# Start of a convolution and SoLU layer: w_in's third block in one transfer, a band mask of one head, two multiplications on GpSimd, and another order of first products, sums and w_out's decode

## The chip, the cores and the metric

The kernel runs on one core of a Trainium2 chip. The core has five engines that each work through their own queue in program order: TensorE (PE: matmuls, with weight loads beside them, PEld), VectorE (DVE), ScalarE (ACT), GpSimd (POOL) and SyncE (SP, which here only issues DMAs). They wait for one another by semaphores. Sixteen DMA engines move data between HBM and the on-chip memory SBUF; matmuls write to PSUM. The metric is the device time of one launch in microseconds, lower is better.

## The reference

The first part is a causal convolution with 7 taps along the sequence, one softmax-normed set of taps for each of 8 heads of 24 channels. The second is a layer of width 1024 with a softmax-gated activation, a layer norm and an output product.

```python
# x [8, 4160, 192], weight [8, 7]
w = exp(weight - max(weight)); w = w / (sum(w) + 1e-09)
out = einsum('hk,bskhg->bshg', w, x_unf)        # 7 taps, causal
# w_in [192, 1024], w_out [1024, 192], g_ln [1024], doubles on entry
h = x @ w_in
e = exp(h - max(h)); sm = e / (sum(e) + 1e-09)
solu = h * sm
ln = (solu - mean(solu)) / sqrt(var(solu) + 1e-06) * g_ln
return ln @ w_out
```

There are 33280 rows, 260 tiles of 128. The weights arrive as 64-bit floats, which the kernel takes apart as pairs of 32-bit words.

## The kernel before

The kernel works on 17 chunks of the sequence (the first of 1024 rows, the second of 1056, the others of 2080) and, in the main loop, on three tiles of 128 rows at once (`three_steps`). For a tile, PE forms ph = y·w_in from fp16 halves (`whi` and `wlo` for w_in, upper and lower y in the transposed tile `yT`). DVE takes the row maximum (`emit_max`), ACT the exponential (`emit_exp`), DVE the numerator (`emit_mul`), ACT the upper half in fp16 (`emit_hi`), POOL the lower half (`emit_lo`), a DMA transposes it into `pT`, and PE multiplies by w_out (`ohl`). All this stands in one program order written by hand: an engine's queue is the order in which the code calls it, and what an engine can't start yet holds up all that is behind it on the same engine.

The change lies in what comes before the main loop:

- **Loads.** SP issues `weight`, then x of chunk 0 (`xr`) and w_in (`raw_in`) in turn. w_in has 192 rows: rows 0 to 127 come in two halves of 512 columns (L383), and rows 128 to 191, the third block, as two transfers over 64 partitions each (L388), side by side in columns 1024 to 1535 of the tile (slice `Z`; the two halves are `halves[0]` and `halves[1]`). Then w_out (`raw_out`, L392).
- **Taps.** POOL makes a 0/1 mask for all heads in `band` (L404, L405), DVE multiplies the taps in (L524), sums, and PE spreads them into `taps`.
- **Decode of 64-bit words** (class `Words`). DVE cuts out exponents (`exponents`, L447) and mantissas (`mantissas`, L452), adds the low word (`join`, L481); ACT turns exponents into powers of two (`powers`, L487) and sums their squares (`squares`, L470); DVE puts in the sign (`signs`, L490), and mantissa times power gives the value (`value`, L497). For w_in all multiplications are on DVE; for w_out the low words (`lows`, L458), the sum (`whole`, L475) and the value (L497) are on POOL, the conversion (`floats`, L464) on ACT.
- **Scales.** PE adds up the squares over partitions (`total`), DVE makes a power of two from the sum: `s` for x (from `xm`), `t_in` for w_in (from `isq`). `cv` holds products of both.
- **Convolution of chunk 0** in two parts: banks `pq` (windows 0 to 4) and `pr` (5 to 9). ACT writes the upper halves y (L313), DVE the lower (L322), and `settle` has SP transpose three blocks into `yT` (L352): block 0 needs uppers alone, block 2 the first two lowers, block 1 all.
- **fp16 halves of w_in.** ACT makes `whi` (L628 for the halves, L644 for the third block), DVE `wlo` (L647).
- **First tiles** (`first_two`, `emit_first`): tiles 0 and 1 share their first products; w_out is decoded between their steps, and `out_powers` multiplies the powers by g_ln on ACT (L685). Then `second_two`: tiles 2 and 3, two convolution products of chunk 1 in the banks of tile 1, w_out's mean over 1024 rows.

The engine of the last step of the decode is an argument:

```python
def value(self, c, powers, eng):
    f = self.f[:, c]
    eng.tensor_tensor(f, f, powers[:, c].bitcast(F32), ALU.mult)
```

Of the kernel before, what the change touches and what calls it, by code (L numbers as in the profile page):

```python
# [19 lines left out]
def kernel(  # L20
# [9 lines left out]
    nc = tc.nc  # L30
# [356 lines left out]
    for j in range(2):  # L387
        nc.sync.dma_start(  # L388
            raw_in[j * R : (j + 1) * R, F:, :].rearrange("p f t -> p (f t)"),
            w_in[2 * R : D, j * F : (j + 1) * F],  # L390
        )
# [12 lines left out]
    pool.memset(band, 1.0)  # L404
    pool.affine_select(  # L405
        out=band, in_=band, pattern=[[0, H], [-1, TB], [-1, K]],
# [101 lines left out]
    def valued(c):  # L508

        wi.signs(c, wi.m)  # L510
        wi.value(c, wi.m, dve)
# [13 lines left out]
        band, band, wb.unsqueeze(2).broadcast_to([TJ, H, TB, K]), ALU.mult  # L525
# [12 lines left out]
    valued(halves[0])  # L538
# [48 lines left out]
    isq = cp.tile([P, 2], F32, name="isq")  # L587
# [45 lines left out]
    wo.lows(W, 2.0**-32)  # L633
    wi.join(Z)
    valued(Z)
    for pc, hg in got0:
        c0.upper(pc, *hg)
# [35 lines left out]
    gate = cp.tile([1, 1], F32, name="gate")  # L673
# [67 lines left out]
    def emit_first(t, u):  # L741
# [4 lines left out]
        for j, w, r in ((0, whi, 0), (2, whi, 0), (0, wlo, 0), (1, whi, 1)):  # L746
            for q, lhs in zip((t, u), y):
                for n, bank in enumerate(banks_of(q)):
                    nc.tensor.matmul(
                        bank, lhs[j], w[:, r, n * 512 : (n + 1) * 512],  # L750
                        start=j == 0 and w is whi, stop=False,
                    )
                for n in range(NH if r else 0):
                    emit_third(q, n, False, False)
# [394 lines left out]
    def first_two():  # L1149
# [4 lines left out]
        emit_exp(t)  # L1154
        wo.signs(W, wo.e)

        pool.tensor_copy(gate, wo.e.bitcast(F32)[0:1, 0:1])
        wo.whole(W)
# [439 lines left out]
```

## Time and profile before

| | before |
|---|---|
| device time, three runs | 1162.87, 1164.15, 1164.42 us |
| median | 1164.15 us |
| profiled execution: span from first to last instruction | 1161.5 us |
| PE busy in the span | 1132.2 us (97%) |
| DVE, ACT, POOL busy | 1016.8, 998.0, 878.6 us |
| DMA: packets, bytes | 727391, 226.95 MB |

The profile is of one execution. Its own whole time is not listed; what is known is its span, and that the timed runs lie 1.4 to 2.9 us above it. In a timeline row stand start and length in us, the engine, the line of the kernel, the operation, what it writes and reads, the shape, how many were merged (x3), and in brackets how long the engine had been idle and what ended that. A row of a table by stretch has the stretch, its length, busy time and number of instructions of PE, PEld, DVE, ACT and POOL, the granted clock of PE (1.00 is full), the share of time the 16 DMA engines were busy and GB/s. "DMA to landing" is from the issue of a transfer to the arrival of its last byte.

### The profile page before, as it was taken

How to read it: one execution, taken by the hardware profiler on the slowest of the kernel's cores; microseconds unless marked ns; L12 is line 12 of the kernel's file. 1: busy time of each engine (PE TensorE's matmuls, PEld its weight loads, DVE VectorE, ACT ScalarE, POOL GpSimd, SP SyncE). 2: the span in 40 equal slices, each digit the busy share in tenths (PEclk: the TensorE clock that was granted, in tenths of full speed). 3: DMA queues.
4: the chain of work that ended last, by engine and by line, in shares of the span. 5: the costliest groups of instructions: out<-in, count | busy, mean ns of one | idle time of the engine just before them, and what ended most of it. 6: DMA issues, size and time to landing. Idle time of an engine off the chain costs nothing.

```text
span 1161.5 us, 22374 instructions
## 1 busy us (share of the span) xinstructions
PE 1132.2 (97%) x7742; PEld 692.4 (60%) x7742; DVE 1016.8 (88%) x2058; ACT 998.0 (86%) x1775; POOL 878.6 (76%) x686
## 2 busy tenths in 40 slices
PE   5898999999999999999999999999999999999998
PEld 3575566656666665655656666665666566566556
DVE  8888898988989898998889989888898988788787
ACT  6998988888888888888888888898888889888886
POOL 2745879987888588887868888588788858855665
PEclk9999999999999999999999999999999999999999
DMA  8799899999999999999999999999999998999988
GB/s 226 171 181 180 185 218 205 205 201 202 200 213 195 195 186 220 207 189 199 202 198 190 208 209 199 187 202 208 206 204 198 195 193 170 174 177 186 181 163 188
DMA packets 727391, 226.95 MB, mean 195 GB/s; under 512 B 651614, under 2 KB 725870, under 8 KB 727278
## 3 DMA queue, kind: packets, MB, share of 16 engines
q1 hardware_dynamic: 727278, 225.53, 100.2%
q8 instruction: 60, 0.98, 0.3%
q14 instruction: 53, 0.43, 0.1%
HBM read 33.00 MB, written 25.56 MB: 50 GB/s over the span
## 4 chain that ended last, share of the span: by engine, by line
PE 88%; DVE 5%; ACT 2%; DMA 2%; issue 2%; POOL 1%; SPq 0%; DVEq 0%; ACTq 0%; POOLq 0%
PE po L859 40%; PE ph L736 36%; PE pc L281 6%; PE ph L759 5%; DVE e L807 1%; DMA pT<-p 1%; DVE ph L790 1%; DMA raw_in<-in_moe_w_in_dram 1%; ACT e L797 1%; ACT sq L819 0%; DVE raw L869 0%; DVE y L322 0%; POOL p L827 0%; PE mean L701 0%; DVE wlo L647 0%
## 5 line engine op out<-in xcount | busy, mean ns | idle before, releaser
L827 POOL TENSOR_TENSOR p<-e,p 128x1024 f16<-128x1024 f32 x257 | 548.3, 2138 | 219.5 <-ACT p L815 218.0
L859 PE MATMUL po<-ohl,pT 128*128 128x192 f16 (+1 forms) x4264 | 539.8, 283 | 7.8 <-DVE raw L869 5.4
L859 PEld LDWEIGHTS <-pT 128*128 128x128 f16 x4264 | 384.4, 98 | 167.1 <-issue 7.6
L736 PE MATMUL ph<-whi,yT 128*128 128x512 f16 x1548 | 419.1, 380 | 2.7 <-DVE e L807 2.6
L790 DVE TENSOR_SCALAR_CACHE_REDUCE ph<-ph,cv 128x1024 f32<-128x1024 f32 x248 | 319.1, 1288 | 72.9 <-PE ph L759 56.6
L797 ACT ACTIVATE e<-ph,sm 128x1024 f32<-128x1024 f32 x260 | 289.4, 1113 | 102.0 <-DVE ph L790 95.8
L807 DVE SCALAR_TENSOR_TENSOR e<-ph,cv,e 128x1024 f32<-128x1024 f32 x248 | 317.1, 1279 | 26.0 <-ACT e L797 25.7
L736 PEld LDWEIGHTS <-yT 128*128 128x128 f16 x2064 | 192.6, 98 | 231.3 <-issue 36.3
L815 ACT CAST p<-e 128x1024 f16<-128x1024 f32 x257 | 266.8, 1039 | 27.9 <-DVE e L807 27.3
L819 ACT ACTIVATE sq<-e 128x1024 f32<-128x1024 f32 x260 | 273.4, 1052 | 0.2
L736 PE MATMUL ph<-wlo,yT 128*128 128x512 f16 x516 | 153.5, 379 | 0.0
L869 DVE TENSOR_REDUCE raw<-po 128x192 f32<-128x384 f32 x247 | 136.3, 552 | 14.3 <-PE po L859 13.9
L243 POOL TENSOR_TENSOR xs<-xr,xs 128x960 f16<-128x960 f32 (+1 forms) x56 | 107.6, 1922 | 1.4
L313 ACT ACTIVATE y<-pc 112x432 f16<-112x432 f32 (+5 forms) x140 | 62.8, 469 | 13.8 <-PE pc L281 8.1
L759 PE MATMUL ph<-wlo,yT 64*128 64x512 f16 x269 | 74.0, 380 | 0.0
L322 DVE SCALAR_TENSOR_TENSOR y<-pc,y 112x432 f16<-112x432 f32 (+5 forms) x140 | 72.2, 532 | 0.8 <-ACT y L313 0.8
L281 PE MATMUL pc<-xs,taps_hi 128*112 128x240 f16 (+1 forms) x448 | 72.9, 261 | 0.0
L759 PE MATMUL ph<-wlo,y 64*128 64x512 f16 x251 | 68.6, 380 | 0.0
L181 DVE TENSOR_REDUCE xa<-xr 128x1 f32<-128x384 f32 x112 | 66.6, 617 | 0.0
L281 PEld LDWEIGHTS <-taps_hi 128*112 128x112 f16 x448 | 52.4, 130 | 16.4
L240 POOL TENSOR_SCALAR xr<-xr,s 128x960 f32<-128x960 f32 (+1 forms) x56 | 57.5, 1027 | 2.9
L281 PE MATMUL pc<-xs,taps_lo 128*112 128x240 f16 (+1 forms) x224 | 58.5, 261 | 0.0
(148 smaller groups left out, 787.6 us busy)
## 6 DMA issues: line engine op xcount, KB each, us to landing
out_dram<-raw SPq DMA_DIRECT2D x127, 192.0 KB, 3.0
xr<-in_x_dram SPq DMA_DIRECT2D x41, 480.0 KB, 4.7
xr<-in_x_dram SPq DMA_DIRECT2D x22, 384.0 KB, 4.1
pT<-p SPq DMA_TRANSPOSE x263, 4.6
y<-yT SPq DMA_DIRECT2D x15, 140.0 KB, 3.1
y<-yT SPq DMA_DIRECT2D x15, 126.0 KB, 3.1
yT<-y SPq DMA_TRANSPOSE x102, 3.7
raw_out<-in_moe_w_out_dram SPq DMA_DIRECT2D x1, 1536.0 KB
```

Of the source, the lines that this page charges most:

```text
L243: (2.1 * size + 0.2, lambda: pool.tensor_tensor(xl, r, h, ALU.subtract)),
L281: nc.tensor.matmul(o, tp[:, h + j, :], r, start=q == 0, stop=q == len(ops) - 1)
L736: nc.tensor.matmul(bank, lhs, w[:, r, n * 512 : (n + 1) * 512], start=start and j == 0, stop=stop and j == len(ops) - 1,)
L759: nc.tensor.matmul(banks_of(t)[n], y[q, t.off : t.off + P], wlo[q, 1, n * 512 : (n + 1) * 512], start=start, stop=not start,)
L790: dve.tensor_scalar(t.ph, t.ph, t.cv[:, 0:1], None, ALU.mult, ALU.min, accum_out=t.bias)
L797: act.activation(t.e, t.ph, AF.Exp, bias=t.bias, scale=-1.0, accum_out=grp.z[:, g : g + 1])
L807: dve.scalar_tensor_tensor(t.e, t.ph, t.cv[:, 3:4], t.e, ALU.mult, ALU.mult, accum_out=t.grp.s1[:, t.g : t.g + 1],)
L815: act.copy(t.p16[:, :, 0, :], t.halves)
L819: act.activation(junk, t.e, AF.Square, accum_out=t.grp.s2[:, t.g : t.g + 1])
L827: eng.tensor_tensor(t.p16[:, :, 1, :], t.halves, t.p16[:, :, 0, :], ALU.subtract)
L859: nc.tensor.matmul(t.po[:, 0:n], t.pT[:, a, :], w, start=j == 0, stop=j == len(ops) - 1)
L869: dve.tensor_reduce(t.grp.raw[:, t.g, :], t.po[:, 0 : 2 * D].rearrange("p (a d) -> p d a", a=2), AX.X, ALU.add,)
```

## The change

The diff, without two lines that only move a declaration:

```diff
-    for j in range(2):
-        nc.sync.dma_start(
-            raw_in[j * R : (j + 1) * R, F:, :].rearrange("p f t -> p (f t)"),
-            w_in[2 * R : D, j * F : (j + 1) * F],
-        )
+    nc.sync.dma_start(
+        raw_in[:, F:, :].rearrange("p f t -> p (f t)"),
+        w_in[2 * R : D, :].rearrange("r (j f) -> j r f", j=2),
+    )
...
-    pool.memset(band, 1.0)
+    mask = sp.tile([TJ, F], F32, name="mask", tag="e", bufs=4)
+    mask = mask[:, 0 : TB * K].rearrange("p (c k) -> p c k", k=K)
+    pool.memset(mask, 1.0)
     pool.affine_select(
-        out=band, in_=band, pattern=[[0, H], [-1, TB], [-1, K]],
+        out=mask, in_=mask, pattern=[[-1, TB], [-1, K]],
...
-    def valued(c):
+    def valued(c, eng=pool):
         wi.signs(c, wi.m)
-        wi.value(c, wi.m, dve)
+        wi.value(c, wi.m, eng)
...
     dve.tensor_tensor(
-        band, band, wb.unsqueeze(2).broadcast_to([TJ, H, TB, K]), ALU.mult
+        band, mask.unsqueeze(1).broadcast_to([TJ, H, TB, K]),
+        wb.unsqueeze(2).broadcast_to([TJ, H, TB, K]), ALU.mult,
     )
...
     wi.powers(halves[0])
-    valued(halves[0])
+    isq = cp.tile([P, 3], F32, name="isq")
+    wi.squares(halves[0], isq[:, 0:1])
+    valued(halves[0], dve)
...
-    wi.squares(A, isq[:, 0:1])
-    wi.signs(halves[1], wi.m)
+    wi.squares(halves[1], isq[:, 1:2])
     wi.exponents(Z)
+    wi.mantissas(Z)
     wi.powers(Z)
     for f in chain0[1:-3]:
         f()
-    wi.squares(Z, isq[:, 1:2])
+    wi.squares(Z, isq[:, 2:3])
+    valued(halves[1])
     for pc, hg in got0:
         c0.upper(pc, *hg)
-    wi.value(halves[1], wi.m, dve)
-    wi.mantissas(Z)
+    wi.join(Z)
...
     for c in halves:
         act.activation(whi[:, 0, c], wi.f[:, c], AF.Copy, scale=t_in)
+    valued(Z)
     settle(*spans0[0], got1)
...
-    wo.lows(W, 2.0**-32)
-    wi.join(Z)
-    valued(Z)
-    for pc, hg in got0:
-        c0.upper(pc, *hg)
...
     wo.exponents(W)
+    for pc, hg in got0:
+        c0.upper(pc, *hg)
     for f in chain0[-3:]:
         f()
-    wo.mantissas(W)
     wo.powers(W)
-    wo.floats(W)
+    wo.lows(W, 2.0**-32)
...
-        for j, w, r in ((0, whi, 0), (2, whi, 0), (0, wlo, 0), (1, whi, 1)):
-            for q, lhs in zip((t, u), y):
...
+        for w in (whi, wlo):
+            for q, lhs in zip((t, u), y):
+                product(q, lhs, 0, w, 0)
+        for q, lhs in zip((t, u), y):
+            product(q, lhs, 2, whi, 0)
+            product(q, lhs, 1, whi, 1)
+            for n in range(NH):
+                emit_third(q, n, False, False)
...
         emit_max(t)
         emit_exp(t)
+        wo.mantissas(W)
+        wo.floats(W)
+        wo.whole(W)
         wo.signs(W, wo.e)
-        pool.tensor_copy(gate, wo.e.bitcast(F32)[0:1, 0:1])
-        wo.whole(W)
```

The mask is made for one head and read by the multiplication for all eight; it borrows a buffer of the exponentials. The squares of w_in are summed in three pieces instead of two. The first products take the y blocks in the order 0 (upper weights), 0 (lower weights), then 2 and 1 of tile 0, then 2 and 1 of tile 1. The one-element copy `gate` on POOL is gone. Line numbers shift by one to five (L497 is now L498, L790 is L795).

Three places show what moved. First DVE, from the join of w_in's second half to the sum of w_in's squares (`isq`). Before:

```order
L481 SCALAR_TENSOR_TENSOR f_in<-raw_in,m_in 128x512
L490 SCALAR_TENSOR_TENSOR m_in<-raw_in,e_in 128x512
L447 TENSOR_SCALAR e_in<-raw_in 128x512
L203 TENSOR_REDUCE xm_166<-pt_x_174 128x1
L105 TENSOR_SCALAR s_167<-xm_166 128x1
L106 TENSOR_SCALAR s_167<-s_167 128x1
L109 TENSOR_SCALAR s_167<-s_167 128x1
L112 TENSOR_SCALAR s_167<-s_167 128x1
L497 TENSOR_TENSOR f_in<-f_in,m_in 128x512
L452 TENSOR_SCALAR m_in<-raw_in 128x512
L624 TENSOR_REDUCE isq<-pt_wi 128x1
```

The same stretch of DVE after the change:

```order
L482 SCALAR_TENSOR_TENSOR f_in<-raw_in,m_in 128x512
L448 TENSOR_SCALAR e_in<-raw_in 128x512
L453 TENSOR_SCALAR m_in<-raw_in 128x512
L203 TENSOR_REDUCE xm_168<-pt_x_176 128x1
L105 TENSOR_SCALAR s_169<-xm_168 128x1
L106 TENSOR_SCALAR s_169<-s_169 128x1
L109 TENSOR_SCALAR s_169<-s_169 128x1
L112 TENSOR_SCALAR s_169<-s_169 128x1
L491 SCALAR_TENSOR_TENSOR m_in<-raw_in,e_in 128x512
L482 SCALAR_TENSOR_TENSOR f_in<-raw_in,m_in 128x512
L627 TENSOR_REDUCE isq<-pt_wi 128x1
```

The block's exponents and mantissas (L448, L453) now stand ahead of the second half's sign step (L491), the block's join stands ahead of the sum for t_in instead of behind the lower halves y, and the multiplication is gone from DVE. The block's sign step follows t_in's four root steps.

Second POOL, from its last constant to the last step of w_out's decode. Before:

```order
L420 MEMSET even 128x128
L458 TENSOR_SCALAR raw_out<-raw_out 128x1536
L208 TENSOR_SCALAR cv_168<-cv_168 128x1 x3
L1157 COPY gate<-e_out 1x1
L475 TENSOR_TENSOR f_out<-m_out,raw_out 128x1536
L497 TENSOR_TENSOR f_out<-f_out,e_out 128x1536
```

The same stretch of POOL after the change:

```order
L421 MEMSET even 128x128
L498 TENSOR_TENSOR f_in<-f_in,m_in 128x512 x2
L208 TENSOR_SCALAR cv_170<-cv_170 128x1 x3
L459 TENSOR_SCALAR raw_out<-raw_out 128x1536
L476 TENSOR_TENSOR f_out<-m_out,raw_out 128x1536
L498 TENSOR_TENSOR f_out<-f_out,e_out 128x1536
```

The two multiplications of w_in come first, and the scaling of w_out's low words has moved from ahead of cv to behind it.

Third DVE again, around the maximum of tile 0 (`ph_273` before, `ph_272` after). Before:

```order
L447 TENSOR_SCALAR e_out<-raw_out 128x1536
L205 TENSOR_SCALAR cv_168<-s_167,t_in 128x1
L117 TENSOR_SCALAR cv_168<-cv_168 128x1
L452 TENSOR_SCALAR m_out<-raw_out 128x1536
L790 TENSOR_SCALAR ph_273,sm_295<-ph_273,cv_168 128x1024
L490 SCALAR_TENSOR_TENSOR e_out<-raw_out,e_out 128x1536
L807 SCALAR_TENSOR_TENSOR e_297,s_0_269<-ph_273,cv_168,e_297 128x1024
```

The same stretch of DVE after the change:

```order
L448 TENSOR_SCALAR e_out<-raw_out 128x1536
L205 TENSOR_SCALAR cv_170<-s_169,t_in 128x1
L117 TENSOR_SCALAR cv_170<-cv_170 128x1
L795 TENSOR_SCALAR ph_272,sm_294<-ph_272,cv_170 128x1024
L453 TENSOR_SCALAR m_out<-raw_out 128x1536
L491 SCALAR_TENSOR_TENSOR e_out<-raw_out,e_out 128x1536
L812 SCALAR_TENSOR_TENSOR e_296,s_0_268<-ph_272,cv_170,e_296 128x1024
```

w_out's mantissas (L453) now stand behind tile 0's maximum (L795).

More of the change, by code (lines that the diff above doesn't have):

```diff
@@ L586 @@
     t_in = cp.tile([P, 1], F32, name="t_in")
-    isq = cp.tile([P, 2], F32, name="isq")
     chain0 = c0.scale_steps()
@@ L670, in settle_rest @@
         nc.sync.dma_start(wlo[low, 1, :], wlo[top, 1, :])
-    gate = cp.tile([1, 1], F32, name="gate")
     o_inv = cp.tile([P, 1], F32, name="o_inv")
@@ L745, in emit_first, with product @@
             q.ph = pair(slot, f"ph_{q.i}")
-        for j, w, r in ((0, whi, 0), (2, whi, 0), (0, wlo, 0), (1, whi, 1)):
-            for q, lhs in zip((t, u), y):
[L748 to L754, printed above, removed]
+        def product(q, lhs, j, w, r):
+            for n, bank in enumerate(banks_of(q)):
+                nc.tensor.matmul(
+                    bank, lhs[j], w[:, r, n * 512 : (n + 1) * 512],
+                    start=j == 0 and w is whi, stop=False,
+                )
+        for w in (whi, wlo):
+            for q, lhs in zip((t, u), y):
+                product(q, lhs, 0, w, 0)
[4 more added lines that the diff above has]
+                emit_third(q, n, False, False)
     def emit_third(t, n, low, start):
```

## The prediction

> **What bounds the kernel now.** I read the busy times by stretch of the span first (length, then PE, weight loads, DVE, ACT and POOL with their instructions, the granted clock, the DMA share and GB/s), to see which part of the program can pass a gain on.
>
> ```profile
> 20.00:30.00 10.00, 6.88 (x27) 2.03 (x26) 9.75 (x14) 7.84 (x11) 2.40 (x5) 1.00 0.95 248
> 90.00:100.00 10.00, 8.20 (x56) 4.85 (x54) 9.27 (x20) 6.51 (x13) 6.16 (x5) 1.00 0.80 138
> 150.00:200.00 50.00, 50.00 (x343) 30.50 (x342) 45.47 (x94) 43.43 (x80) 45.05 (x42) 1.00 1.03 213
> ```
>
> From 150 us on PE (first busy figure after the length) never rests: from there the time is a fixed queue of products, which ends earlier exactly as much as it starts earlier. Before 30 us PE is the one that waits (6.88 of 10), and DVE is busy for 9.75. Every instruction that the change touches lies in those first 37 us, so the question is only how much earlier the queue starts. That is read from DVE's timeline (start, length, line).
>
> ```profile
> 11.43 0.43 DVE L447 TENSOR_SCALAR e_in<-raw_in 128x512 int32<-128x512 int32 x1 [0.56 <-DMA raw_in<-in_moe_w_in_dram]
> 13.03 0.69 DVE L490 SCALAR_TENSOR_TENSOR m_in<-raw_in,e_in 128x512 int32<-128x512 int32 x1
> 14.80 0.68 DVE L497 TENSOR_TENSOR f_in<-f_in,m_in 128x512 f32<-128x512 f32 x1
> 16.05 0.16 DVE L624 TENSOR_REDUCE isq<-pt_wi 128x1 f32<-128x2 f32 x1 [0.23 <-PE pt_wi L95]
> 16.81 0.15 DVE L112 TENSOR_SCALAR t_in<-t_in 128x1 int32<-128x1 int32 x1
> 16.88 1.46 DVE L322 SCALAR_TENSOR_TENSOR y<-pq,s,y 112x480 f16<-112x480 f32 x3
> 18.25 1.28 DVE L481 SCALAR_TENSOR_TENSOR f_in<-raw_in,m_in 128x512 f32<-128x512 uint32 x1
> 20.91 2.84 DVE L647 SCALAR_TENSOR_TENSOR wlo<-f_in,t_in,whi 128x512 f16<-128x512 f32 x4
> 24.97 0.97 DVE L452 TENSOR_SCALAR m_out<-raw_out 128x1536 int32<-128x1536 int32 x1
> 25.84 1.30 DVE L790 TENSOR_SCALAR_CACHE_REDUCE ph<-ph,cv 128x1024 f32<-128x1024 f32 x1
> 27.04 1.77 DVE L490 SCALAR_TENSOR_TENSOR e_out<-raw_out,e_out 128x1536 int32<-128x1536 int32 x1
> 28.92 1.28 DVE L807 SCALAR_TENSOR_TENSOR e<-ph,cv,e 128x1024 f32<-128x1024 f32 x1
> 33.09 1.28 DVE L807 SCALAR_TENSOR_TENSOR e<-ph,cv,e 128x1024 f32<-128x1024 f32 x1 [0.28 <-ACT e L797]
> ```
>
> From the landing of w_in's second half at 11.43 DVE runs almost without a gap to the numerators of tile 0 (28.92) and tile 1 (33.09). What follows hangs on these two.
>
> ```profile
> 30.27 0.60 PE L736 MATMUL ph<-whi,yT 128*128 128x512 f16 x2 [1.69 <-DVE e L807]
> 34.48 2.98 PE L281 MATMUL pc<-xr,taps 128*112 128x120 f32 x16 [1.77 <-issue]
> 29.08 2.88 ACT L685 ACTIVATE e_out<-e_out,gl 128x192 f32<-128x192 f32 x8 [0.26 <-POOL gate L1157]
> 31.86 1.10 ACT L797 ACTIVATE e<-ph,sm 128x1024 f32<-128x1024 f32 x1
> ```
>
> The convolution at 34.48 takes tile 1's banks, free at 34.38 when its numerator ends. That numerator waits for ACT's exponential (31.86), which stands behind eight multiplications with g_ln (29.08). So I count the start of ACT's row 29.08: whatever that gains, tile 1, the convolution and the queue behind it gain.
>
> **The mask.** A select over 20x98 replaces one over 20x784.
>
> ```profile
> 2.53 1.29 DVE L516 TENSOR_TENSOR wb<-wb,wtop 20x56 f32<-20x56 f32 x1
> 5.14 0.20 DVE L523 TENSOR_TENSOR wb<-wb,wtop 20x56 f32<-20x56 f32 x1
> 1.66 2.23 POOL L405 TENSOR_SCALAR_AFFINE_SELECT band<-band 20x784 f32<-20x784 f32 x1
> ```
>
> The same DVE shape takes 1.29 us while POOL selects and 0.20 later, so DVE wins 1.1 us at the start. The select's new length lies between 0 and 2.23; a value near an eighth, 0.3, is taken, and it decides nothing: DVE already waits 0.56 at 11.43 for w_in's second half, and will now wait longer. Nothing is counted. The new squares of the first half on ACT (about 0.8) go into the same gap.
>
> **The third block in one transfer.** DVE now wants the block right behind the second half's join. Before, the sign step followed that join at 13.03, about 0.1 of it a wait for ACT; so at 12.90.
>
> ```profile
> L388 SPq DMA_DIRECT2D raw_in<-in_moe_w_in_dram x1: 588/588/588, 4.3 to 4.3; - x1
> DMA to landing us min/median/max: 9.1/9.1/9.1
> 8.00:9.00 1.00, 1.00 (x12) 1.00 (x12) 0.96 (x3) 0.68 (x1) 0.00 (x0) 1.00 1.04 352
> 10.00:11.00 1.00, 0.37 (x2) 0.37 (x3) 0.84 (x2) 1.00 (x4) 0.00 (x0) 1.00 0.92 197
> ```
>
> Its second part lands at 4.3 + 9.1 = 13.4. At 10 us the DMA engines are as busy as at 8 (0.92 against 1.04), yet move 197 GB/s instead of 352: the time of the two 64-partition parts. 512 KB at 197 GB/s is 2.7 us, at 352 it is 1.5. I take the gain of 1.2: it lands at 12.2 and costs no wait. The bounds are 12.2 and the 13.4 of now, which would hold DVE 0.5. The Trainium skill, SBUF — State Buffer, section "Can I just issue two DMAs to hit both halves?", says that two transfers over 64 partitions each serialize and only one over 128 reaches all ports. By it the block comes early; kept at 13.4, the sum shrinks by the 0.5 of a rival below.
>
> **Decode and scale of w_in.** Before, 13.03 to 14.80 held the second half's sign step (0.65), the block's exponents, and the sum and roots of s. Now 12.90 starts the same without the sign step and with the block's mantissas (0.43): to 14.45. Then the signs of the second half (0.65) to 15.10, the join of the block (0.65) to 15.75, and the scale t_in (16.05 to 16.9 before) to 16.6. So t_in is 0.3 earlier than before. Then comes the block's sign step, and here POOL stands in the way. It multiplies the second half from 15.8 on.
>
> ```profile
> 32.76 3.44 POOL L497 TENSOR_TENSOR f_out<-f_out,e_out 128x1536 f32<-128x1536 f32 x1
> 17.42 1.59 POOL L458 TENSOR_SCALAR raw_out<-raw_out 128x1536 f32<-128x1536 uint32 x1 [12.56 <-DMA raw_out<-in_moe_w_out_dram]
> 24.95 1.03 POOL L208 TENSOR_SCALAR cv<-cv 128x1 f32<-128x1 f32 x1 [5.95 <-DVE cv L205]
> 54.82 0.61 POOL L208 TENSOR_SCALAR cv<-cv 128x1 f32<-128x1 f32 x3
> ```
>
> A third of the 128x1536 product is 1.15 us (bounds 0.68, DVE's own, and 3.44). DVE and POOL exclude each other in some steps: DVE's join at 18.25 took 1.28 instead of 0.69 while POOL ran to 19.01, and POOL's first cv step took 1.03, where three take 0.61 elsewhere, while DVE's mantissas ran (24.97 to 25.94). The steps with two SBUF inputs and the fast single-input ones exclude POOL; those that read PSUM do not (1.30 at 25.84). So the sign step waits until 16.95, and the lower halves y start at 17.6, **0.7 late**. From there DVE is ahead: no join with its 1.28, no sign step, no multiplication stands between them and wlo, which starts at 17.6 + 1.37 = 18.97 (was 20.91) and ends at 21.85. Exponents of w_out and cv, which took from 23.75 to 24.97, follow to 23.1.
>
> **First products.** The y transposes go out 0.7 late.
>
> ```profile
> 17.91 2.51 SPq L352 DMA_TRANSPOSE yT<-y  x2
> DMA to landing us min/median/max: 2.5/2.5/2.5
> 24.01 0.59 PE L749 MATMUL ph<-whi,yT 128*128 128x512 f16 x2 [0.84 <-ACT whi L644]
> 24.54 0.60 PE L759 MATMUL ph<-wlo,yT 64*128 64x512 f16 x2
> ```
>
> The last block, second of these two issues (19.2), landed at 21.7; now 22.4. PE waited longer, to 24.01, for whi's third block; POOL's second product (17.6 to 18.75) lets ACT make it from 18.8 to 21.75, so the transposition now ends last. Tile 0's last four products take 24.01 to 25.14, so 1.13: it is complete at 23.55, and DVE's maximum starts there instead of 25.84, because the mantissas of w_out also stand behind it now. On ACT the exponential, now ahead of the mantissas' conversion, starts about 24.9 and is hidden.
>
> **What is given back.** POOL's scaling of w_out's low words no longer has the empty stretch at 17.42: it follows cv, 23.1 + 0.61 to about 25.35. DVE's maximum (PSUM) does not mind, but the mantissas at 24.75 do: they wait to 25.35. Bounds: no wait, or 1.6 if POOL started just ahead. Then 0.85 for them and 1.88 for the signs: 28.1. The Trainium skill, SBUF — State Buffer, section "Who interferes with whom", has this as an exclusive lock which the first keeps for its whole instruction. By it 0.6 is lost here; without it the sum would be 0.6 better.
>
> **The sum.** Numerator of tile 0: 28.1 against 28.92, 0.8 earlier. ACT's g_ln products also lose POOL's gate copy (0.27): 28.05 against 29.08, **1.03 earlier**. Exponential and numerator of tile 1, and the convolution, follow by the same 1.03. POOL's two w_out steps (3.5 and 3.44) ended at 36.2; now they start at 28.05, when the signs release the lock, and end at 35.1, still ahead of the convolution's end at 36.4, so the mean is not held up. Behind that all engines have the orders of before, and the end comes 1.0 earlier: a span of 1160.5 instead of 1161.5. The profiled execution's own whole time is not listed; the median of the three timed runs is 2.65 above its span. With that kept, I predict 1163.1 us.
>
> **Rivals.**
>
> ```profile
> 35.00:36.00 1.00, 1.00 (x8) 1.00 (x7) 1.00 (x3) 1.00 (x2) 1.00 (x1) 0.52 0.69 140
> 41.94 1.80 ACT L715 ACTIVATE ohl<-f_out,t_out 128x768 f16<-128x768 f32 x2 [0.70 <-DVE f_out L710]
> 15.87 1.87 PE L281 MATMUL pr<-xr,taps 128*112 128x120 f32 x16
> 81.00 6.57 DMA pT<-p
> pT<-p SPq DMA_TRANSPOSE x263, 4.6
> ```
>
> *Clock, or no lock.* Behind a pause of PE the granted clock is about half (0.52 at 35 us) on the convolution and part of the mean: its sixteen products take 2.98 us, the same sixteen at 15.87 take 1.87. If the moved pauses put this elsewhere, PE gains 1.1 there and perhaps 0.6 on the mean; ACT, which waits 0.70 at 41.94, passes on 0.7. That makes 1.7, so 1162.4; without POOL's 0.6 as well 1161.8, and 1160.8 if all of PE's gain came through. For it: the pauses move. Against: they stay about as long. The Trainium skill, TensorE: Matmul & The Clock Gate, Part 1, says that the gate's window runs free of the kernel's start; by that the stretch would come and go between executions of either kernel, which one trace cannot show.
>
> *POOL takes its turn first.* If the second half's product starts before the block's join, join and t_in go back 1.2, but the sign step no longer waits (0.35): 0.85 lost, 0.2 left, 1163.9. Against: DVE's next step starts before the last has left (24.97, POOL's cv blocked).
>
> *The transfer does nothing.* Landing at 13.4: 0.5 lost, 1163.6.
>
> *Slower.* Between 80 and 130 us PE is not full (8.20 of 10), and the chain of waits has a transposition pT that took 6.57 us where the median is 4.6. If the shift lays one more such transposition against an x load there, 2.0 are lost and 1.0 over: 1165.1. It decides from the first one that is late by more than 1.0. Against: loads and transpositions stand in one queue and shift together.
>
> **How the numbers follow.** Forecast 0.42 (1162.6 to 1163.6, by the 0.5 around each stall), clock or no lock 0.25, POOL first 0.10, transfer 0.10, slower 0.13. The range takes in these cases with their bounds, 1160.8 to 1165.2. A measurement tells about 0.2% (2.3 us) from no change: below 1161.8 lies only the far part of the second case, 0.15; above 1166.5 only two late transpositions, 0.04; within, 0.81.
>
> **What would show it.** Right: the block's exponents near 12.9 without a wait, lower halves y about 17.6, tile 0's maximum about 23.5, w_out's mantissas held to the end of POOL's scaling, g_ln products about 28. Wrong: a wait of the exponents for DMA, the joins or the sign step longer than 0.7, POOL's product ahead of the join, or a gain at 34 us that is gone at 150.

## The result, and the profile after

| | before | after |
|---|---|---|
| device time, median | 1164.23 us (5 runs, 1162.87 to 1164.62) | 1170.93 us (5 runs, 1169.07 to 1172.21) |
| ratio, 95% interval | 1 | 1.0065 [1.0052, 1.0077] |
| span of the profiled execution | 1161.5 us | 1169.7 us |

The change makes the kernel 6.7 us slower by the medians, where 1.0 us faster was forecast; the forecast's range ended at 1165.2. (The ratio is not the quotient of the two medians, which is 1.0058; by it the loss is 7.6 us, 6.1 to 9.0 by its interval.) The chain of waits of after (start, length, what ran or was waited for) says at once where:

```profile
3.71 17.74 DMA raw_in<-in_moe_w_in_dram
21.47 0.43 DVE e_in L448
```

From the issue of the one transfer at 3.71 to DVE's first step on the block the chain is nothing but this load. The table by stretch shows what the load did in that time.

```profile
9.00:10.00 1.00, 0.41 (x2) 0.41 (x3) 0.97 (x3) 1.00 (x4) 0.00 (x0) 1.00 1.03 345
15.00:20.00 5.00, 0.00 (x0) 0.00 (x0) 0.00 (x0) 0.00 (x0) 0.00 (x0) 1.00 0.13 52
22.00:25.00 3.00, 1.54 (x7) 1.54 (x8) 2.72 (x13) 2.63 (x6) 1.25 (x1) 1.00 0.13 46
```

For five microseconds no engine does anything at all, and the share of the DMA engines stands at 0.13: of 16 engines two are busy (0.13 x 16 = 2.1), and they move 52 GB/s. w_out, issued behind the block at 4.4, landed 21.1 later, at 25.5, and between the two landings the share is still 0.13. The trace doesn't name the engines. That w_out's last part waited on the same two is an estimate: two sixteenths of its 1536 KB are 192 KB, at the 46 GB/s of the last row 4.3 us, and from 21.47 to 25.5 it is 4.0.

```profile
L391 SPq DMA_DIRECT2D raw_out<-in_moe_w_out_dram x1: 467/467/467, 4.4 to 4.4; - x1
DMA to landing us min/median/max: 21.1/21.1/21.1
```

In before DVE had used the block at 13.64.

```profile
13.64 0.42 DVE L447 TENSOR_SCALAR e_in<-raw_in 128x512 int32<-128x512 int32 x1
```

In the timelines of DVE, POOL, ACT and PE after the change all that follows is late.

```profile
9.67 0.42 DVE L448 TENSOR_SCALAR e_in<-raw_in 128x512 int32<-128x512 int32 x1
21.47 0.43 DVE L448 TENSOR_SCALAR e_in<-raw_in 128x512 int32<-128x512 int32 x1 [10.32 <-DMA raw_in<-in_moe_w_in_dram]
24.93 0.15 DVE L112 TENSOR_SCALAR t_in<-t_in 128x1 int32<-128x1 int32 x1
25.00 0.94 DVE L491 SCALAR_TENSOR_TENSOR m_in<-raw_in,e_in 128x512 int32<-128x512 int32 x1
25.86 1.46 DVE L322 SCALAR_TENSOR_TENSOR y<-pq,s,y 112x480 f16<-112x480 f32 x3
31.95 1.29 DVE L795 TENSOR_SCALAR_CACHE_REDUCE ph<-ph,cv 128x1024 f32<-128x1024 f32 x1 [0.58 <-PE ph L764]
33.16 1.12 DVE L453 TENSOR_SCALAR m_out<-raw_out 128x1536 int32<-128x1536 int32 x1
35.86 1.28 DVE L812 SCALAR_TENSOR_TENSOR e<-ph,cv,e 128x1024 f32<-128x1024 f32 x1
39.99 1.28 DVE L812 SCALAR_TENSOR_TENSOR e<-ph,cv,e 128x1024 f32<-128x1024 f32 x1 [0.25 <-ACT e L802]
23.75 1.64 POOL L498 TENSOR_TENSOR f_in<-f_in,m_in 128x512 f32<-128x512 f32 x1 [21.28 <-DVE m_in L491]
31.86 1.61 POOL L459 TENSOR_SCALAR raw_out<-raw_out 128x1536 f32<-128x1536 uint32 x1
35.99 2.88 ACT L684 ACTIVATE e_out<-e_out,gl 128x192 f32<-128x192 f32 x8
41.39 2.34 PE L281 MATMUL pc<-xr,taps 128*112 128x120 f32 x16 [1.73 <-issue]
```

DVE waited 10.32 for the block. Tile 1's numerator starts at 39.99 instead of 33.09, 6.9 late, and the median is 6.7 higher (7.6 by the ratio): within the scatter, the queue of products behind it passes the delay on whole. In the two profiled executions DVE's reductions (the operation of L795) are 6.9 late up to 142 us and the last one 7.4, and the spans differ by 8.2.

### The profile page after: what moved, and what is told of

Its sections match the earlier page's. It is cut to its first block, busy times and chain, and to the rows that moved or that the text cites. A ratio compares the mean times of both kernels' runs of the same rounds, so it can differ in the third digit from the quotient of the medians.

```text
span 1169.7 us, 22371 instructions
## 1 busy us (share of the span) xinstructions
PE 1134.3 (97%) x7742; PEld 693.7 (59%) x7742; DVE 1013.5 (87%) x2056; ACT 997.8 (85%) x1777; POOL 877.7 (75%) x687
## 4 chain that ended last, share of the span: by engine, by line
PE 88%; DVE 4%; DMA 3%; ACT 2%; issue 2%; POOL 1%; SPq 0%; POOLq 0%; ACTq 0%; DVEq 0%
PE po L864 40%; PE ph L735 36%; PE pc L281 6%; PE ph L764 5%; DMA raw_in<-in_moe_w_in_dram 2%; DMA pT<-p 1%; DVE e L812 1%; DVE ph L795 1%; POOL p L832 1%; ACT sq L824 1%; ACT e L802 0%; ACT p L820 0%; PE mean L700 0%; DVE y L322 0%; ACT y L313 0%
## 5 line engine op out<-in xcount | busy, mean ns | idle before, releaser
L795 DVE TENSOR_SCALAR_CACHE_REDUCE ph<-ph,cv 128x1024 f32<-128x1024 f32 x248 | 319.1, 1288 | 74.2 <-PE ph L764 57.8
L281 PEld LDWEIGHTS <-taps_hi 128*112 128x112 f16 x448 | 52.5, 130 | 16.4
```

The source lines that it names most:

```text
L281: nc.tensor.matmul(o, tp[:, h + j, :], r, start=q == 0, stop=q == len(ops) - 1)
L795: dve.tensor_scalar(t.ph, t.ph, t.cv[:, 0:1], None, ALU.mult, ALU.min, accum_out=t.bias)
```

## The experiments

Three theories stood at first. **A**: the source of the new transfer is written as two column halves, each of 64 rows, so its slowest dimension has two steps, and only as many DMA engines share in it; the rest of the change does about what was forecast. **B**: one transfer of this size, in this place, is slow in itself. **C**: other edits cost too. Each run is timed against the kernel before on the same chip; the ratio is to it, with its 95% interval.

**e1_two: the change with the block in two transfers again.**

```diff
-    nc.sync.dma_start(raw_in[:, F:, :]..., w_in[2 * R : D, :].rearrange("r (j f) -> j r f", j=2))
+    for j in range(2):
+        nc.sync.dma_start(raw_in[j * R : (j + 1) * R, F:, :]..., w_in[2 * R : D, j * F : (j + 1) * F])
```

> The changed kernel with w_in's third block loaded by two transfers over 64 partitions again; all other edits stay. Theory A (the block's one transfer is worked by two DMA engines only, because the slowest dimension of its source has two steps, and nothing else in the change costs): the block lands at about 13.4 us as before, DVE takes its exponents without a wait of 10 us, tile 0's maximum starts near 24 instead of 31.95, and the whole is 0.5 us faster than before (ratio 0.9996, between 0.998 and 1.0005). Theory C (the other edits cost too: the multiplications on GpSimd, the late scaling of w_out's low words): slower than before, ratio 1.001 or more, with the wait of the mantissas or of the sign step over 1.5 us.

Measured: 1163.33 us, ratio 0.9996 [0.9986, 1.0007]. The whole loss is in this one edit; C falls. DVE's timeline shows the two waits that are left:

```profile
11.68 0.43 DVE L449 TENSOR_SCALAR e_in<-raw_in 128x512 int32<-128x512 int32 x1 [1.91 <-DMA raw_in<-in_moe_w_in_dram]
13.88 0.43 DVE L449 TENSOR_SCALAR e_in<-raw_in 128x512 int32<-128x512 int32 x1 [0.71 <-DMA raw_in<-in_moe_w_in_dram]
17.40 0.94 DVE L492 SCALAR_TENSOR_TENSOR m_in<-raw_in,e_in 128x512 int32<-128x512 int32 x1
32.46 1.28 DVE L813 SCALAR_TENSOR_TENSOR e<-ph,cv,e 128x1024 f32<-128x1024 f32 x1 [0.25 <-ACT e L803]
```

**e2_before_one: the kernel of before with only the one transfer.** The first hunk of the change, alone:

```diff
-    for j in range(2):
-        nc.sync.dma_start(raw_in[j * R : (j + 1) * R, F:, :]..., w_in[2 * R : D, j * F : (j + 1) * F])
+    nc.sync.dma_start(raw_in[:, F:, :]..., w_in[2 * R : D, :].rearrange("r (j f) -> j r f", j=2))
```

> The kernel before with only the third block's load changed to one transfer. Theory A: the block lands at about 21 us, w_out at about 25, and DVE's exponents of the block, at 13.64 before, start at 21.5; the scale of x stands behind them, so all later work is about 7.8 us late, and the whole 7 to 8 us slower (ratio 1.006 to 1.007). Theory C: half of the loss or less (ratio under 1.0035), the rest being due to the other edits.

Measured: 1171.76 us, ratio 1.0075 [1.0061, 1.0089], a little above A's 1.006 to 1.007. The edit carries its loss into the other kernel: DVE waits 8.50 for the block at 21.73, with the same share and rate.

```profile
15.00:20.00 5.00, 0.00 (x0) 0.00 (x0) 0.00 (x0) 0.00 (x0) 0.00 (x0) 1.00 0.13 52
21.73 0.43 DVE L446 TENSOR_SCALAR e_in<-raw_in 128x512 int32<-128x512 int32 x1 [8.50 <-DMA raw_in<-in_moe_w_in_dram]
```

**e3_rows: one transfer of the same bytes, in memory order.** The slowest dimension of the source now has 128 steps.

```diff
-        w_in[2 * R : D, :].rearrange("r (j f) -> j r f", j=2),
+        w_in[2 * R : D, :].rearrange("r (j f) -> (r j) f", j=2),
```

> The changed kernel with its one transfer written with the 128 source pieces in the order of memory, so that the slowest dimension has 128 steps; the block's pieces then stand in other partitions, so the products with it use exchanged rows of w_in, while every instruction stays. Theory A: the transfer is spread over all engines, lands between 10 and 13 us, DVE waits for it under 1 us, and the whole is 0.5 to 1.5 us faster than before (ratio 0.9987 to 0.9996). Theory B (one transfer of this size behind the others is slow in itself, sharing with w_out's transfer that follows it): it lands at about 21 us again and the whole is as slow as the changed kernel (ratio 1.006).

Measured: 1160.60 us, ratio 0.9981 [0.9971, 0.9991]. This separates A from B: one transfer, the same bytes, the same place, and the block is used at 12.02 without a wait. From 9 to 12 us, with other loads in flight too, all 16 engines are busy, at 384 GB/s; in after two were busy from 15 to 20, at 52. That is 24 GB/s for each of 16 and 26 for each of two. The engines are not slow; too few of them take part.

```profile
9.00:12.00 3.00, 1.45 (x7) 1.45 (x8) 2.83 (x6) 2.97 (x9) 0.00 (x0) 1.00 1.03 384
12.02 0.42 DVE L448 TENSOR_SCALAR e_in<-raw_in 128x512 int32<-128x512 int32 x1
16.06 0.68 DVE L491 SCALAR_TENSOR_TENSOR m_in<-raw_in,e_in 128x512 int32<-128x512 int32 x1
22.76 1.29 DVE L795 TENSOR_SCALAR_CACHE_REDUCE ph<-ph,cv 128x1024 f32<-128x1024 f32 x1 [0.58 <-PE ph L764]
23.97 1.23 DVE L453 TENSOR_SCALAR m_out<-raw_out 128x1536 int32<-128x1536 int32 x1
30.90 1.28 DVE L812 SCALAR_TENSOR_TENSOR e<-ph,cv,e 128x1024 f32<-128x1024 f32 x1 [0.25 <-ACT e L802]
```

It came out faster than A's range: tile 1's numerator is 2.19 earlier than before, and 0.19% of 1163.6 is 2.2 us (the medians differ by 3.0).

**e4_four: e3_rows with four source groups.**

```diff
-        w_in[2 * R : D, :].rearrange("r (j f) -> (r j) f", j=2),
+        w_in[2 * R : D, :].rearrange("r (j f) -> (r j) f", j=2).rearrange("(i g) f -> g i f", g=4),
```

> As the run before, but with the source pieces taken in four groups, so that the slowest dimension has four steps (the pieces again stand in other partitions). Theory A: four DMA engines work on it; the stretch in which only this transfer is left shows a DMA share of 0.25 and about 100 GB/s instead of 0.13 and 49, and the block lands between 14 and 17 us. Theory B: landing and share are those of the changed kernel (21 us, 0.13).

Measured: 1168.56 us in one run. The share doubles to 0.27 (4.3 engines) and the rate to 98 GB/s, as A has it. The landing, 19.0, is 2 us later than A's range; why is not settled.

```profile
18.00:20.00 2.00, 0.00 (x0) 0.00 (x0) 0.96 (x4) 0.54 (x1) 0.00 (x0) 1.00 0.27 98
19.00 0.43 DVE L448 TENSOR_SCALAR e_in<-raw_in 128x512 int32<-128x512 int32 x1 [6.91 <-DMA raw_in<-in_moe_w_in_dram]
```

So A stands. The Trainium skill, DMA: Bandwidth & Descriptors, section "Why a DMA increments its semaphore by 16 and not by 1", states it as a rule: the number of engines is the largest up to 16 that divides the slowest dimension of both sides. Shares of 0.13, 0.27 and 1.03 with 2, 4 and 128 steps agree with it.

**e7_y_first: the change, with the block's steps behind everything that doesn't need it.** Does the late block cost so much because it stands in DVE's queue ahead of the x scale?

```diff
     wi.squares(halves[1], isq[:, 1:2])
+    for f in chain0[1:-3]:
+        f()
+    valued(halves[1])
+    for pc, hg in got0:
+        c0.upper(pc, *hg)
+    c0.open(0, None)
+    settle(*spans0[0], got0)
     wi.exponents(Z)
     wi.mantissas(Z)
     wi.powers(Z)
-    for f in chain0[1:-3]:
-        f()
     wi.squares(Z, isq[:, 2:3])
-    valued(halves[1])
-    for pc, hg in got0:
-        c0.upper(pc, *hg)
     wi.join(Z)
-    c0.open(0, None)
...
-    settle(*spans0[0], got1)
```

> The changed kernel, block in its one transfer, but the x scale, the upper and lower halves y with their transpositions, and the second half's values stand ahead of the block's five steps on DVE, so that only what needs the block waits for it. Theory A (the block lands at about 21.5 whatever stands ahead of it, and t_in needs it): exponents of the block at 21.5 as before, t_in 24.4 to 24.7 (24.93), lower halves y at 15 to 16 (25.86), tile 0's maximum at 29.5 to 30.5 (31.95), its numerator at 33.5 to 34.5 (35.86); ratio 1.0045 to 1.0058 against 1.0065 of the changed kernel. If the place of the block in DVE's order were the whole loss, and not the landing itself: maximum at 25 to 26, ratio 0.999 to 1.001.

Measured: 1170.40 us, ratio 1.0068 [1.0055, 1.0081]. The landing is the loss, not the place: y was done at 16.4, yet tile 0's maximum starts at 31.51 (31.95 in after), since t_in, and with it whi and wlo, needs the block. A's expected gain of 1.5 to 2.5 at the maximum was too high, and the ratio lies above its 1.0045 to 1.0058: wlo, taken at 2.84, took 3.81 while POOL's product ran (25.84 to 27.11).

```profile
21.63 0.43 DVE L448 TENSOR_SCALAR e_in<-raw_in 128x512 int32<-128x512 int32 x1 [5.21 <-DMA raw_in<-in_moe_w_in_dram]
25.95 3.81 DVE L645 SCALAR_TENSOR_TENSOR wlo<-f_in,t_in,whi 128x512 f16<-128x512 f32 x4 [0.19 <-ACT whi L631]
25.84 1.27 POOL L498 TENSOR_TENSOR f_in<-f_in,m_in 128x512 f32<-128x512 f32 x1 [11.20 <-DVE m_in L491]
```

**e5_queues: the two transfers from two engines.**

```diff
+    third_block(nc.sync, 0)
...
     act.activation(wb, wb, AF.Exp)
+    third_block(act, 1)
```

> The changed kernel with the third block again as two transfers over 64 partitions each, the first issued by SP in its old place, the second by ACT behind its exponential of the taps (about 3.2 us), so that both are in flight together instead of one behind the other. In e1_two, one behind the other on SP, the block was there at 13.9 and w_in's second half at 11.7, with DVE waiting 0.71 and 1.91; in e3_rows, as one transfer over 128 partitions, at 12.0 and before 10.6, with no wait. Theory S (a part over 64 partitions is slow because it uses half of SBUF's side, so two in flight together make up for one another): both arrive as in e3_rows, the block by 12.5, DVE waits under 0.3 for the two, tile 0's numerator starts at 27.0 or before, ratio 0.9980 to 0.9987. Theory T (they share one set of engines and take the same time in sum whatever queue they come from, as the Trainium skill, SBUF - State Buffer, section on two DMAs for both halves, says): the block at 13.5 to 14, numerator at 28.2 to 28.6, ratio 0.9992 to 1.0000.

Measured: 1164.34 us, ratio 1.0016 [1.0006, 1.0025]. S falls: the dip in the rate is still there at a full share, and the second half is there at 12.39, later than in e1_two (11.68).

```profile
11.00:12.00 1.00, 0.59 (x4) 0.33 (x2) 0.00 (x0) 0.74 (x2) 0.00 (x0) 1.00 1.03 204
12.39 0.43 DVE L451 TENSOR_SCALAR e_in<-raw_in 128x512 int32<-128x512 int32 x1 [2.70 <-DMA raw_in<-in_moe_w_in_dram]
```

The sentence of the Trainium skill that the prediction names (SBUF — State Buffer, section "Can I just issue two DMAs to hit both halves?"), that two such transfers serialize, agrees.

T holds by its places: the block is used at 13.80 without a wait, tile 0's numerator starts at 28.23. It misses by the ratio, 0.9992 to 1.0000 expected. The run is slower than before although tile 1's numerator starts 0.75 earlier (32.34). In the profiled execution a lead of 0.6 is left at DVE's last reduction, and the end still comes 0.6 later than in before: from there to the end it takes 6.6, before 5.4. Why is open, and so is whether the other runs lose it there too.

**e6_sign: e1_two, with the second half's sign and product ahead of the block.**

```diff
     wi.squares(halves[1], isq[:, 1:2])
+    wi.signs(halves[1], wi.m)
+    wi.value(halves[1], wi.m, pool)
     wi.exponents(Z)
...
     wi.squares(Z, isq[:, 2:3])
-    valued(halves[1])
```

> The changed kernel with the block in two transfers as in e1_two, and the second half's sign step and GpSimd product put ahead of the block's exponents, so that the sign step (0.69) fills DVE's wait of 0.71 for the block. Theory A (the rest of the change works as its steps say, the start of the lower halves y is set by DVE's work behind the block): the block's exponents still at 13.9, t_in and the block's sign step 0.69 earlier, POOL's product done before the sign step, which takes 0.69 instead of 0.94; lower halves y at 17.3 instead of 18.26, numerator of tile 1 at 31.6 instead of 32.46, ratio 0.9987 to 0.9993. Theory L (DVE and POOL exclude each other, and POOL's product now comes between the block's exponents and the x scale): one of DVE's steps there, or POOL's product ahead of them, costs 0.6 to 1.3, lower halves y at 17.9 to 18.6, ratio 0.9994 to 1.0000.

Measured: 1162.88 us, ratio 1.0001 [0.9990, 1.0012]. L holds by its places, with the lower halves y at 18.34; the ratio is 0.0001 above its range. The block was there at 13.54, but DVE's step on it takes 1.39 instead of 0.43 and ends 0.3 after POOL's product, which ends at 14.64.

```profile
13.54 1.39 DVE L449 TENSOR_SCALAR e_in<-raw_in 128x512 int32<-128x512 int32 x1 [0.24 <-DMA raw_in<-in_moe_w_in_dram]
13.38 1.26 POOL L499 TENSOR_TENSOR f_in<-f_in,m_in 128x512 f32<-128x512 f32 x1 [10.91 <-DVE m_in L492]
```

**e9_order: e6_sign, with w_in's second half issued ahead of x's second part.**

```diff
+    chunks[0].load(0)
     for j in range(NH):
-        chunks[0].load(j)
         nc.sync.dma_start(raw_in[:, j * 512 : (j + 1) * 512, :]..., w_in[0 : 2 * R, j * F : (j + 1) * F])
+    chunks[0].load(1)
```

> As e6_sign (block in two transfers, the second half's sign step and GpSimd product ahead of the block's exponents), and SP issues w_in's second half ahead of the second part of x instead of behind it. In e1_two x's second part was used by ACT at 9.45 and the second half arrived at 11.68; they should change places, while the block still arrives at 13.5 to 13.9. In e6_sign the product ran on GpSimd from 13.38 to 14.64 and the block's exponents took 1.39 instead of 0.43 beside it. Theory L (the 0.96 was the exclusion of DVE and POOL, not a slow load): the second half's exponents at 9.7 to 10.3, its product ends on GpSimd by 13.5, the block's exponents take 0.43 again when the block is there, 13.5 to 13.9; lower halves y at 17.2 to 17.5 (18.34 in e6_sign, 18.26 in e1_two), numerator of tile 1 at 31.4 to 31.7, ratio 0.9984 to 0.9993. If the 0.96 was something else, or if the x scale now waits for x's second part, the exponents take over 1 us again or the x scale comes after 15.0, lower halves y at 18 or later, ratio 0.9994 to 1.0002.

Measured: 1163.86 us, ratio 1.0001 [0.9990, 1.0012], a miss: the x scale came at 15.25 and the lower halves y at 18.09, as the other case had it. The trace still speaks for the exclusion. The sign step now waited for ACT, so the product met the block's mantissas instead, which took 1.50 for 0.42, while the exponents ahead of them took their 0.42.

```profile
13.83 1.50 DVE L455 TENSOR_SCALAR m_in<-raw_in 128x512 int32<-128x512 int32 x1
13.67 1.38 POOL L500 TENSOR_TENSOR f_in<-f_in,m_in 128x512 f32<-128x512 f32 x1 [11.19 <-DVE m_in L493]
```

**e11_powers: e9_order, with ACT's powers of the second half ahead of the squares of x's second part.**

```diff
     words(halves[1])
+    wi.powers(halves[1])
     for h in c0.halves(1):
         c0.sum_squares(*h)
-    wi.powers(halves[1])
```

> As e9_order, and ACT makes the second half's powers ahead of the squares of x's second part instead of behind them, so that the second half's sign step needn't wait for ACT: in e9_order it waited 2.01 for it, to 12.89, and the product on GpSimd (13.67, 1.38) again met the block's steps, one of which took 1.50 instead of 0.42. Theory L (exclusion of DVE and POOL): sign step at 10.8 to 11.2, product on GpSimd from 11.5 to 12.8, all of it while DVE waits for the block; the block's exponents and mantissas at 13.5 to 13.9 take 0.43 and 0.42; x scale from 14.2 to 14.5, lower halves y at 17.0 to 17.3 instead of 18.09, wlo at 18.4 to 18.7, tile 0's maximum at 23.1 to 23.4 and tile 1's numerator at 31.3 to 31.5 instead of 24.17 and 32.32; ratio 0.9985 to 0.9996. If the two steps were long for another reason: one of them over 1 us again, lower halves y at 18 or later, ratio 0.9995 to 1.0005.

Measured: 1162.86 us, ratio 0.9998 [0.9987, 1.0008]. POOL's product ran from 12.09, while DVE waited, and the block's two steps took 0.43 and 0.42: third evidence for the exclusion. The gain didn't come. In the profiled execution the block landed only at 15.6, after a wait of 3.61; but that execution is the slowest of the 12 (1165.85), so it doesn't tell why the others show no gain either.

```profile
15.62 0.43 DVE L450 TENSOR_SCALAR e_in<-raw_in 128x512 int32<-128x512 int32 x1 [3.61 <-DMA raw_in<-in_moe_w_in_dram]
12.09 1.26 POOL L500 TENSOR_TENSOR f_in<-f_in,m_in 128x512 f32<-128x512 f32 x1 [9.62 <-DVE m_in L493]
```

**e10_before_order: the kernel of before with that order of loads.** 

```diff
+    chunks[0].load(0)
     for j in range(NH):
-        chunks[0].load(j)
         nc.sync.dma_start(raw_in[:, j * 512 : (j + 1) * 512, :]..., w_in[0 : 2 * R, j * F : (j + 1) * F])
+    chunks[0].load(1)
```

> The kernel of before with only that order of SP's loads: w_in's second half ahead of x's second part. It tells whether e9_order's gain is the order alone. Before, DVE waited 0.56 at 11.43 for the second half and 0.1 more at 13.03. Expected: the wait of 0.56 goes, since the second half arrives by 10.3 and DVE is free at 10.87; the block is wanted 0.56 earlier, at 13.1, and arrives at 13.4, so about 0.3 of it comes back as a wait for the block; lower halves y at 16.5 to 16.7 instead of 16.88, ratio 0.9994 to 1.0003. If the order alone carries a gain: ratio 0.9990 or below.

Measured: 1164.72 us, ratio 1.0005 [0.9995, 1.0014]: no gain from the order. The wait of 0.56 went, but the sign step behind it waited 1.21 for ACT, whose powers now stood behind the later part of x; lower halves y came at 17.55, not at 16.5 to 16.7.

**e8_dve: e3_rows with all multiplications on DVE.**

```diff
-    def valued(c, eng=pool):
+    def valued(c, eng=dve):
```

> As e3_rows (one transfer of the block over 128 partitions in memory order, the pieces in other partitions, so the output is not the reference's), with all three multiplications of w_in on DVE again instead of two on GpSimd. It measures what the move to GpSimd is worth when no load is late. Theory A (DVE's own time sets the start of the lower halves y and wlo): two products of 0.69 on DVE, one ahead of t_in's steps and one ahead of the lower halves y, so these at 18.0 instead of 16.66, wlo at 19.4 instead of 18.03, maximum of tile 0 at 24.0 to 24.2 instead of 22.76, numerator at 28.0 instead of 26.75, ratio 0.9985 to 0.9994 against 0.9981. Theory L (the exclusion takes back what DVE saves): maximum and numerator within 0.4 of e3_rows, ratio 0.9978 to 0.9984.

Measured: 1163.11 us, ratio 1.0000 [0.9990, 1.0010], above both ranges. The maximum is at 23.60 and the two numerators 0.60 and 0.57 later than in e3_rows. DVE began the second half's sign step 0.73 earlier here (12.87 against 13.60), so from that step to tile 0's numerator it took 1.33 more, in three parts:

- Up to the lower halves y 4.08 against 3.06, 1.02 more: about the two products of 0.69, less the 0.35 for which e3_rows' t_in waited for PE. That is theory A.
- From there to the maximum 0.55 more, since DVE waited longer for PE (1.13 against 0.58), whose granted clock from 19 to 23 us was 0.59 here and 1.00 in e3_rows. No run shows that the edit brings this about.
- From the maximum to the numerator 0.24 less: w_out's mantissas took 0.96 instead of 1.23, since POOL's scaling had ended before them. That is theory L, which takes back a quarter of the 1.02.

So the trace gives the move to GpSimd about 0.8 of the 2.2 us that the two ratios differ by; the rest stays open.

```profile
12.87 0.68 DVE L491 SCALAR_TENSOR_TENSOR m_in<-raw_in,e_in 128x512 int32<-128x512 int32 x1
16.95 1.46 DVE L322 SCALAR_TENSOR_TENSOR y<-pq,s,y 112x480 f16<-112x480 f32 x3
23.60 1.29 DVE L795 TENSOR_SCALAR_CACHE_REDUCE ph<-ph,cv 128x1024 f32<-128x1024 f32 x1 [1.13 <-PE ph L764]
27.35 1.28 DVE L812 SCALAR_TENSOR_TENSOR e<-ph,cv,e 128x1024 f32<-128x1024 f32 x1
```

**e12_before_rows: the kernel of before with e3_rows' transfer.**

```diff
-    for j in range(2):
-        nc.sync.dma_start(raw_in[j * R : (j + 1) * R, F:, :]..., w_in[2 * R : D, j * F : (j + 1) * F])
+    nc.sync.dma_start(raw_in[:, F:, :]..., w_in[2 * R : D, :].rearrange("r (j f) -> (r j) f", j=2))
```

> The kernel of before with only the block in one transfer over 128 partitions in memory order, as in e3_rows (its pieces stand in other partitions, so the output is not the reference's). It tells how much of e3_rows' 0.9981 is the load alone, without the other edits. Before, DVE waited 0.56 for the second half at 11.43 and some 0.1 at 13.03, and wanted the block at 13.60, 0.2 after it had landed. Theory A (only waits that DVE really has can be gained): no wait for either, lower halves y at 16.2 to 16.4 instead of 16.88, tile 0's numerator at 28.3 to 28.5 instead of 28.92, ratio 0.9990 to 0.9998. If the load alone makes e3_rows' gain: tile 0's numerator at 27 or before, ratio 0.9978 to 0.9986.

Measured: 1162.68 us, ratio 0.9996 [0.9985, 1.0007], within A's range. Its places were off by a little: the lower halves y at 16.57 (a wait of 0.25 for ACT), tile 0's numerator at 28.01 and tile 1's at 32.17. Of the gain, 0.31 is there at the lower halves y. The other 0.60 is DVE's join of the block, which took 0.68 instead of 1.28: w_out landed earlier, so POOL's scaling of it (15.35 to 16.95, before 17.42 to 19.01) no longer met the join. The good load alone brings 0.92 at tile 1's numerator (33.09), the other edits alone 0.63 (e1_two), both together 2.19 (e3_rows). With the edits alone DVE waits 0.71 for the block, and with the load alone it wants it only at 13.13; with both it is used at 12.02.

A version that computes everything and is measurably faster than the kernel before was not found. The load of e3_rows puts the rows of one column half into every second partition, and the steps behind it read that half as 64 partitions in one piece; rewriting these was not tried.

## Why the prediction was wrong

**The step that failed** is in "The third block in one transfer": "I take the gain of 1.2: it lands at 12.2 and costs no wait. The bounds are 12.2 and the 13.4 of now". It was there at 21.47, where DVE wanted it at 11.15. The price was the bytes by a rate of the profile (512 KB at 352 GB/s); with 52 GB/s they take 10 us. I had read the halved rate of the 64-partition parts as the only way a load can be slow, and took the landing of before as the worst case. But 13.4 belonged to another access pattern: a new one has no upper bound from the old one's time. Every large load at the start of before has at least 64 rows in its outermost dimension; the one new thing in this transfer was that it has two. The rule of the Trainium skill weighed at that place (one transfer over 128 partitions reaches all ports) agrees with e3_rows (384 GB/s, against 201 with two parts), but it is about the side of SBUF; the rule on the number of engines, named above, spoke against the change and was missed. The rival "the transfer does nothing" shared the error: no case of mine had the block later than 13.4, and what was left above 1165.2 was for late transpositions.

**The other steps, point by point.**

- *The queue from 150 us on passes the start on.* Right within the scatter: 6.9 at tile 1's numerator in after and 6.7 (medians) or 7.6 (ratio) at the end, 2.19 in e3_rows and 3.0 or 2.2.
- *The mask.* Right in kind: DVE's first product on the weights takes 0.20 instead of 1.29. "It decides nothing" was right for the two transfers: in e1_two DVE waits 1.91 for the second half. But "Nothing is counted" hid that this wait, too, came with the 64-partition parts. With the good load the second half is used at 10.63 without one (in e8_dve, where DVE came earlier, at 9.97 after 0.36).
- *Block to lower halves y.* Forecast 4.7 (12.90 to 17.6); after took 4.39, e3_rows 4.64.
- *POOL's product* (1.15, bounds 0.68 and 3.44): 1.26 alone, 1.64 beside DVE's join. It began with the join of the block, not ahead of it, so "POOL takes its turn first" didn't occur; in e6_sign, where it could, it did, and cost 0.96.
- *The block's sign step held 0.35.* It was held 0.26 (0.94 for 0.68) in after and e1_two, and not in e3_rows, where t_in waited 0.35 for PE and POOL had ended by then.
- *y to tile 0's maximum.* Forecast 5.95 (17.6 to 23.55); after took 6.09, e3_rows 6.10.
- *Mantissas of w_out held 0.6 by POOL's scaling.* Mis-sized: held 0.16 in after (1.12 against 0.96) and 0.27 in e3_rows. The scaling began with the maximum and took 1.6 to 1.7, so it ended soon after it. Maximum to numerator took 3.91 and 3.99 instead of 4.55.
- *The sum.* With the block at 21.47 instead of 12.90, 8.57 are to be added to 1163.1; the steps behind it took 0.63 less up to tile 1's numerator. That gives 1171.0, and the median was 1170.93. That it fits to 0.1 is luck: the runs scatter by 3 us, and the ratio gives 1171.8. Put in the landing of e3_rows and the sum is better than forecast, not worse. One term was wrong by 8.57, and the others together by 0.6.
- *Clock or no lock.* The exclusion exists (e6_sign, e9_order, e11_powers), at less than half the price in sum here: 0.26 and 0.16 in after, where 0.35 and 0.6 were counted. The clock is taken up below. *Slower* by a late transposition: no trace shows one between 80 and 130 us (what is lost there goes with the half clock, below), and e3_rows' lead, 2.19 at 31 us, is 2.9 at DVE's last reduction.

## What to carry to other kernels

Before two transfers are merged into one, write down the access pattern of the merged one from its slowest dimension: if that has two steps, two of the 16 DMA engines carry it, and the load behind it may wait too, as w_out did here. In a profile this reads as a DMA share of 0.13 with all engines idle; a rate in GB/s taken from another transfer doesn't price it. And a step moved to another engine may save time only if what is then waited for, here a load, is early too: with all the other edits the late load left 0.9996 (e1_two), the early one 0.9981 (e3_rows). The move alone, with the late load, was not tried.

## What else the runs showed of the hardware

- With the block in two parts over 64 partitions the DMA engines move half as much at a full share: 201 GB/s at 1.01 from 10 to 12 us in e1_two, 384 at 1.03 from 9 to 12 in e3_rows. The parts also hold back the 128-partition load issued ahead of them, which in e1_two was there at 11.68 and in e3_rows by 10.63. That 64 partitions are the cause is not shown: in after, where no transfer is that narrow, the rate falls as well (239 GB/s at 1.08 from 12 to 13 us, with the block on two engines).
- The stretch of about half clock wanders between executions. In before it lay on 33 to 39 us (clock 0.72), in e1_two on 90 to 95, and in the profiled execution of e10_before_order nowhere in the start:

```profile
33.00:39.00 6.00, 4.52 (x24) 4.55 (x25) 5.04 (x12) 6.00 (x10) 6.00 (x3) 0.72 0.51 107
33.00:39.00 6.00, 5.15 (x37) 4.79 (x38) 5.42 (x14) 6.00 (x11) 6.00 (x3) 1.00 0.93 173
90.00:95.00 5.00, 5.00 (x23) 2.93 (x23) 4.51 (x10) 2.71 (x6) 3.55 (x3) 0.67 1.05 166
33.00:39.00 6.00, 4.45 (x34) 4.43 (x34) 5.63 (x13) 6.00 (x11) 6.00 (x3) 1.00 0.65 112
```

  The first row is before, the next two e1_two, the last e10_before_order, whose span was 1159.9 though its median is above that of before. What the stretch costs moves with it: e1_two's lead at DVE's reductions is 0.63 at 34 us, 2.0 from 55 to 96, where before has had its stretch and e1_two not yet, and 0.4 at 99. The gain of the rival *Clock* was there and was given back.

  Of the 96 runs of the kernel before that were timed beside the experiments, the 13 with a mean clock of 1.000 took 1162.1 us on average, the 37 with 0.998 or less 1164.0. So a part of the scatter goes with the clock, though single runs stray from it (one with 0.995 took 1161.75), and a single execution's span can't carry a difference of 1 us. e3_rows' lead is there at equal clock: its four runs with 1.000 took 1159.4 us on average, the four of before beside it 1161.9. Why the stretch wanders was not tried.
